# Key sums and query numerators over rows of four heads with both signs

## Chip, cores and metric

The kernel runs on one core of one Trainium2 chip. The metric is the device time of one execution in microseconds (us). Names of engines are those of the profile: PE (TensorE, matrix products; PEld are its weight loads), DVE (VectorE), ACT (ScalarE), POOL (GpSimd) and SP (SyncE, whose queue issues most transfers).

## The reference

Two mixers act on the same 2048 tokens of width 512, and a gate blends them. The diff touches mixer A, a linear attention with 32 heads of 16 channels.

```python
q, k, v = ...                  # x @ wqkv, split into 32 heads of 16
pq = einsum('bhsd,hdf->bhsf', q, w_phi)          # likewise pk from k
phi_q = concat([softmax(pq), softmax(-pq)], -1)  # 32 features; likewise phi_k
kv = einsum('bhsf,bhsd->bhfd', phi_k, v)         # summed over all tokens
z  = einsum('bhsf->bhf', phi_k)
num = einsum('bhqf,bhfd->bhqd', phi_q, kv)
den = einsum('bhqf,bhf->bhq', phi_q, z)[..., None] + 1e-06
a = (num / den) heads side by side @ wo
# mixer B: z = gelu(x @ w_in); z1, z2 = halves; z2 = layernorm(z2)
# b = (z1 * (w_sp @ z2 + b_sp)) @ w_out
out = g * a + (1 - g) * b      # g = sigmoid(sum(x * gate_w)), one per token
```

Every feature is a softmax over 16 values, once of the projection and once of its negative; key features are summed against v over all tokens before any query can be answered.

## The kernel before

Tokens come in NT = 16 tiles of 128. The order of work on every engine is the order of the program, written out by hand; tiles are followed by semaphores only. PSUM is one array ps of eight banks of 512 f32 columns, and the bank numbers are chosen by hand.

**First stage.** For each token tile, PE computes x @ w_in (z_piece, L174), ACT applies gelu, DVE takes the layer norm's statistics. In between come v_proj (v for a token tile, tokens on partitions, copied by ACT into vv) and fold, which multiplies w_phi into the q and k weights, so that wq and wk yield pq and pk at once. wv's columns are reordered first, heads innermost (permute_wv).

**First loop, i = 0 to 15.** gg_half(i) is one half of a spatial tile of mixer B: 16 matmuls of 344 columns (L370) into bank i % 2, which DVE multiplies into u (L378); after each second half, SP issues a transpose of u by DMA into uT, and a load of a further w_sp tile. k_norm(i) sums the exponentials ek of a token tile over the 16 values of each head (L319), inverts (L325), and multiplies v by the inverses, once for each sign (L327): it is v that is scaled, and ek stays as it is. kv_acc(i - 1) accumulates, for both signs and four groups of eight heads, 128 feature rows by 128 v columns and 8 sums of weights: eight matmuls of 136 columns (L343), in banks 3 to 5. k_proj(i + 2) computes pk of a token tile and both exponentials (L307, L312, L313). In the last four iterations q_proj yields pq for four token tiles at once, features on partitions (L397), with its exponentials.

**Second loop, j = 0 to 15.** One more gg_half, in all but the last two, which share one. q_num(j) uses q's exponentials as stationary operand against kvx, the masked key sums: eight matmuls of 144 columns (L417), of which 8 + 8 columns for each sign and group are q's own softmax sums and the denominators' parts. Twelve DVE instructions (L425 to L455) combine signs, denominators and gate into o, tokens on partitions; SP issues its transpose into oT (L457). out_tile(j - LAG), with LAG = 4, multiplies uT (L463) and oT (L468) by w_out and wo, ACT copies (L472), and SP issues the store (L473). The last tile is done in two halves.

Between the loops stand one gg_half, the last kv_acc and kv_extract (L348). That turns the sums in PSUM into kvx, with everything outside a head's own block masked away. A bank is written again only when its reader is done: gg_half's u, the exponentials, kv_extract, and in the second loop q_num's DVE instructions.

Of the kernel before, what the change touches and what calls it, by code (L numbers as in the profile page):

```python
# [37 lines left out]
def kernel(  # L38
# [47 lines left out]
    wv_n = pers.tile([P, NDT, D], BF16, name="wv_n")  # L86
# [9 lines left out]
    warm = vv[:, 13, :]  # L96
    nc.vector.memset(warm[:, 0:P], 0.0)
# [7 lines left out]
    xn = vv[:, 14:16, :]  # L105
# [12 lines left out]
        out=wv_n[:, :, :],  # L118
# [181 lines left out]
    KBANK = (2, 6)  # L300
    ek_t = {}
    vr_t = {}

    def k_proj(t):
        b = KBANK[t % 2]
        for dt in range(NDT):
            nc.tensor.matmul(  # L307
                ps[:, b, :], lhsT=xT[:, dt, t * P:(t + 1) * P], rhs=wk[:, dt, :],
                start=(dt == 0), stop=(dt == NDT - 1),
            )  # L310
# [4 lines left out]

    def k_norm(t):
        ek = ek_t[t]
        zk = ring2.tile([P, 2 * NDT, 8], FP32, name="zk")
        nc.vector.tensor_reduce(  # L319
            out=zk[:], in_=ek[:].rearrange("p a (g h f) -> p (a g) h f", g=NDT, h=8),  # L320
            axis=AX.X, op=ALU.add,
        )
        vr = ring2.tile([P, 2 * NDT, VW], BF16, name="vr")
        with nc.allow_low_precision(reason="the normalised feature is bf16 in the reference"):
            nc.vector.reciprocal(out=vr[:, :, P:VW], in_=zk[:])  # L325
        for a in range(2):
            nc.vector.tensor_tensor(  # L327
                out=vr[:, a * NDT:(a + 1) * NDT, 0:P].rearrange("p g (d h) -> p g d h", h=8),
                in0=vv[:, t, :].rearrange("p (g d h) -> p g d h", g=NDT, h=8),
                in1=vr[:, a * NDT:(a + 1) * NDT, None, P:VW].to_broadcast([P, NDT, DH, 8]),  # L330
                op=ALU.mult,
            )
        vr_t[t] = vr
# [4 lines left out]

    def kv_acc(t):
        ek, vr = ek_t.pop(t), vr_t.pop(t)  # L340
        for j in range(2 * NDT):
# [1 line left out]
            nc.tensor.matmul(  # L343
                kv_slot(j), lhsT=ek[:, a, g * P:(g + 1) * P], rhs=vr[:, j, :],
                start=(t == 0 and j % 3 == 0), stop=(t == NT - 1), skip_group_check=True,
            )

    def kv_extract():  # L348
        for b in range(3):
            n = 3 if b < 2 else 2  # L350
            acc = ps[:, 3 + b, 0:n * VW].rearrange("p (n w) -> p n w", w=VW)
            j = 3 * b
            nc.vector.scalar_tensor_tensor(
                out=kvx[:, j:j + n, P:VW], in0=acc[:, :, P:VW], scalar=0.5 * DEN_EPS,
                in1=mask16[:, None, :].to_broadcast([P, n, 8]), op0=ALU.add, op1=ALU.mult,
            )
            for i in range(n):
                nc.vector.tensor_tensor(
                    out=kvx[:, j + i, 0:P].rearrange("p (h d) -> p h d", h=8),
                    in0=acc[:, i, 0:P].rearrange("p (d h) -> p h d", h=8),  # L360
                    in1=mask16[:, :, None].to_broadcast([P, 8, DH]), op=ALU.mult,
                )
# [26 lines left out]
    def e_buf(c):  # L389
        if c % 2 == 0:  # L390
            return wqkT[:].rearrange("p (a g) n -> p a g n", a=2)
        return vv[:, 0:8, :].rearrange("p (a g) n -> p a g n", a=2)

    def q_proj(c, g):
        e = e_buf(c)
        for dt in range(NDT):
# [8 lines left out]
    oT_t = {}

    def n_slot(a, g):
        if g < 3:
            return ps[:, 3 + a, g * QW:(g + 1) * QW]
        return ps[:, 5, a * QW:(a + 1) * QW]  # L410

    def q_num(t):
        c, i = divmod(t, CH // P)
        e = e_buf(c)
        for g in range(NDT):
            for a in range(2):
                nc.tensor.matmul(  # L417
                    n_slot(a, g), lhsT=e[:, a, g, i * P:(i + 1) * P],
                    rhs=kvx[:, a * NDT + g, :], start=True, stop=True,
                )  # L420
        main = ps[:, 3:5, 0:3 * QW].rearrange("p a (g w) -> p a g w", w=QW)
        last = ps[:, 5, 0:2 * QW].rearrange("p (a w) -> p a w", w=QW)
        sd = ring2.tile([P, 2, NDT, 16], FP32, name="sd")
        for a in range(2):
            nc.vector.tensor_copy(out=sd[:, a, 0:3, :], in_=main[:, a, :, P:QW])  # L425
        nc.vector.tensor_copy(out=sd[:, :, 3, :], in_=last[:, :, P:QW])
        tw = ring2.tile([P, 4, NDT, 8], FP32, name="tw")
        for a in range(2):
            nc.vector.tensor_tensor(
                out=tw[:, a], in0=sd[:, a, :, 0:8], in1=sd[:, 1 - a, :, 8:16], op=ALU.mult  # L430
            )
        nc.vector.tensor_tensor(out=tw[:, 2], in0=tw[:, 0], in1=tw[:, 1], op=ALU.add)
        nc.vector.reciprocal(out=tw[:, 3], in_=tw[:, 2])
        w = ring2.tile([P, 2, NDT, 8], FP32, name="w")
        for a in range(2):
            nc.vector.scalar_tensor_tensor(
                out=w[:, a], in0=sd[:, 1 - a, :, 8:16], scalar=gate[:, t:t + 1],
                in1=tw[:, 3], op0=ALU.mult, op1=ALU.mult,
            )
        pr = ring2.tile([P, 2, D], BF16, name="pr")  # L440
        for a in range(2):
            nc.vector.tensor_tensor(  # L442
                out=pr[:, a, 0:3 * P].rearrange("p (g h d) -> p g h d", g=3, d=DH),
                in0=main[:, a, :, 0:P].rearrange("p g (h d) -> p g h d", d=DH),
                in1=w[:, a, 0:3, :, None].to_broadcast([P, 3, 8, DH]),
                op=ALU.mult,
            )
        nc.vector.tensor_tensor(
            out=pr[:, :, 3 * P:D].rearrange("p a (h d) -> p a h d", d=DH),
            in0=last[:, :, 0:P].rearrange("p a (h d) -> p a h d", d=DH),  # L450
            in1=w[:, :, 3, :, None].to_broadcast([P, 2, 8, DH]),
            op=ALU.mult,
        )
# [133 lines left out]
```

## Time and profile before

| | us |
|---|---|
| median of three runs (217.18 to 217.5) | 217.28 |
| profiled execution, whole | 217.18 |
| its span, first to last instruction | 215.4 |
| PE busy | 209.2 |
| DVE busy | 152.1 |
| ACT busy | 81.3 |
| first stage, until the first gg_half | 0 to 61 |
| first loop and kv_acc(15) | 61 to 124 |
| second loop and the last tiles | 124 to 215.4 |

Busy shares are averages over these stages. In the profile's groups a row names line, engine, operation, output and inputs, shape and count; behind the bar stand busy us and the mean ns of one, and behind the second bar the idle time before, with what ended it. A matmul's recorded duration contains its way through the array; the pitch from one matmul to the next is shorter and is read from the chain or the timeline. The granted PE clock is 0.998 of full speed as a mean.

### The profile page before, as it was taken

What the parts mean: (1) busy time and instruction counts of PE and PEld (TensorE: products, weight loads), DVE (VectorE), ACT (ScalarE), POOL (GpSimd) and SP (SyncE); (2) the same over time, 40 slices, a digit from 0 to 9 for tenths busy, and PEclk for the clock granted to TensorE, in tenths of its full rate; (3) what the DMA queues carried; (4) which work ended last, traced back from release to release, by engine and by line L of the source; (5) the groups of instructions that cost most, each with busy time, mean ns of one, the idle gap of its engine ahead of it and who ended that gap; (6) DMA issues with size and microseconds to landing.
All of it is one profiled execution on the core that took longest, in us unless ns stands there. A gap on an engine that the chain in (4) does not pass through costs nothing.

```text
span 215.4 us, 3615 instructions
## 1 busy us (share of the span) xinstructions
PE 209.2 (97%) x1364; PEld 125.2 (58%) x1388; DVE 152.1 (71%) x462; ACT 81.3 (38%) x141; POOL 1.9 (1%) x13
## 2 busy tenths in 40 slices
PE   7999999999999999999999999999999999999994
PEld 6355555554456666666656666655555665565543
DVE  2279757395969887878777799997666666679900
ACT  2356676865773242424245222322332223311222
POOL 3000000000000000000000000000000000000000
PEclk9999999999999999999999999999999999999999
DMA  6999999990001464646338261422312313242341
GB/s 188 262 212 212 188 210 201 189 283 18 0 3 37 97 137 75 97 101 134 64 73 134 47 123 27 84 56 59 87 49 55 82 49 62 49 73 64 91 117 52
DMA packets 73441, 22.30 MB, mean 103 GB/s; under 512 B 67744, under 2 KB 73424, under 8 KB 73424
## 3 DMA queue, kind: packets, MB, share of 16 engines
q1 hardware_dynamic: 72208, 21.48, 47.9%
q10 hardware_dynamic: 1216, 0.59, 1.0%
q8 instruction: 11, 0.18, 0.4%
q14 instruction: 6, 0.05, 0.1%
HBM read 3.44 MB, written 2.10 MB: 26 GB/s over the span
## 4 chain that ended last, share of the span: by engine, by line
PE 92%; DMA 3%; DVE 1%; issue 1%; SPq 1%; ACT 0%
PE ps L370 34%; PE ps L174 16%; PE ps L463 10%; PE ps L266 6%; PE ps L307 6%; PE ps L468 6%; PE ps L397 6%; PE ps L417 4%; PE ps L343 4%; DMA w_in<-in_B_w_in_dram 3%; PE ps L293 1%; DVE pr L442 0%; DVE u L378 0%; SPq L110 0%; SPq L108 0%
## 5 line engine op out<-in xcount | busy, mean ns | idle before, releaser
L370 PE MATMUL ps<-zz,wsp 128*128 128x344 bf16 x512 | 80.1, 309 | 0.1
L370 PEld LDWEIGHTS <-wsp 128*128 128x128 bf16 x512 | 50.1, 98 | 28.9
L174 PE MATMUL ps<-w_in,xT 128*128 128x512 bf16 (+1 forms) x188 | 39.5, 360 | 0.7 <-DMA w_in<-in_B_w_in_dram 0.5
L378 DVE SCALAR_TENSOR_TENSOR u<-ps,bcol,zz 128x344 bf16<-128x344 f32 x32 | 18.4, 575 | 27.8 <-PE ps L370 27.7
L174 PEld LDWEIGHTS <-xT 128*128 128x128 bf16 x192 | 18.5, 99 | 19.1 <-DMA w_in<-in_B_w_in_dram 1.0
L199 ACT ACTIVATE zz<-ps 128x1376 bf16<-128x1376 f32 (+2 forms) x18 | 21.4, 1190 | 20.8 <-PE ps L174 20.8
L208 DVE BATCH_NORM_STATS2 stats<-zz 128x6 f32<-128x344 bf16 x32 | 14.9, 507 | 15.0 <-ACT zz L199 15.0
L463 PE MATMUL ps<-w_out,uT 128*128 128x512 bf16 (+1 forms) x100 | 23.4, 366 | 0.1
L312 ACT ACTIVATE ek<-ps 128x512 bf16<-128x512 f32 x16 | 9.6, 598 | 34.5 <-PE ps L307 34.4
L472 ACT ACTIVATE ob<-ps 128x512 bf16<-128x512 f32 (+1 forms) x17 | 9.7, 572 | 29.7 <-PE ps L468 22.1
L319 DVE TENSOR_REDUCE zk<-ek 128x64 f32<-128x1024 bf16 x16 | 19.3, 1209 | 0.0
L307 PE MATMUL ps<-wk,xT 128*128 128x512 bf16 x57 | 15.9, 379 | 0.4
L442 DVE TENSOR_TENSOR pr<-ps,w 128x384 bf16<-128x384 f32 x32 | 16.2, 549 | 0.0
L468 PE MATMUL ps<-wo,oT 128*128 128x512 bf16 (+1 forms) x65 | 16.1, 366 | 0.1
L397 PE MATMUL ps<-xT,wq 128*128 128x512 bf16 x58 | 15.8, 379 | 0.3
L463 PEld LDWEIGHTS <-uT 128*128 128x128 bf16 x102 | 9.8, 98 | 10.0
L266 PE MATMUL ps<-wv,xT 128*128 128x512 bf16 x62 | 15.5, 379 | 0.1
L402 ACT ACTIVATE vv<-ps 128x512 bf16<-128x512 f32 x8 | 4.8, 598 | 25.7 <-PE ps L397 25.7
L327 DVE TENSOR_TENSOR vr<-vv,vr 128x512 bf16<-128x512 bf16 x32 | 12.2, 422 | 0.6
L402 ACT ACTIVATE wqkT<-ps 128x512 bf16<-128x512 f32 x8 | 4.8, 599 | 17.4 <-PE ps L397 17.4
L468 PEld LDWEIGHTS <-oT 128*128 128x128 bf16 x68 | 6.7, 98 | 7.2
L343 PE MATMUL ps<-vr,ek 128*128 128x136 bf16 x128 | 10.2, 223 | 0.0
(62 smaller groups left out, 182.9 us busy)
## 6 DMA issues: line engine op xcount, KB each, us to landing
out_dram<-ob SPq DMA_DIRECT2D x15, 128.0 KB, 1.9
w_out<-in_B_w_out_dram SPq DMA_DIRECT2D x1, 640.0 KB, 5.7
w_in<-in_B_w_in_dram ACTq DMA_DIRECT2D x2, 256.0 KB, 3.8
w_in<-in_B_w_in_dram SPq DMA_DIRECT2D x1, 512.0 KB, 5.4
wv_n<-in_A_wqkv_dram SPq DMA_DIRECT2D x1, 512.0 KB, 6.0
wo<-in_A_wo_dram SPq DMA_DIRECT2D x1, 512.0 KB, 6.0
w_in<-in_B_w_in_dram SPq DMA_DIRECT2D x1, 352.0 KB, 6.8
vv<-in_A_x_dram SPq DMA_DIRECT2D x2, 128.0 KB, 3.1
```

The lines of the kernel that those rows point to most:

```text
L174: nc.tensor.matmul(zb[:, n0:n1], lhsT=xT[:, dt, t * P:(t + 1) * P], rhs=w_in[:, dt, n0:n1], start=(dt == 0), stop=(dt == NDT - 1),)
L199: nc.scalar.activation(out=zz[:, t, n0:n1], in_=zbank(t)[:, n0:n1], func=AF.Gelu_apprx_tanh)
L266: nc.tensor.matmul(ps[:, b, :], lhsT=xT[:, dt, t * P:(t + 1) * P], rhs=wv[:, dt, :], start=(dt == 0), stop=(dt == NDT - 1),)
L307: nc.tensor.matmul(ps[:, b, :], lhsT=xT[:, dt, t * P:(t + 1) * P], rhs=wk[:, dt, :], start=(dt == 0), stop=(dt == NDT - 1),)
L319: nc.vector.tensor_reduce(out=zk[:], in_=ek[:].rearrange("p a (g h f) -> p (a g) h f", g=NDT, h=8), axis=AX.X, op=ALU.add,)
L343: nc.tensor.matmul(kv_slot(j), lhsT=ek[:, a, g * P:(g + 1) * P], rhs=vr[:, j, :], start=(t == 0 and j % 3 == 0), stop=(t == NT - 1), skip_ ...
L370: nc.tensor.matmul(ps[:, b, 0:HF], lhsT=wsp[:, tt % WSLOTS, s, :], rhs=zz[:, s, FH + h * HF:FH + (h + 1) * HF], start=(s == 0), stop=(s == ...
L378: nc.vector.scalar_tensor_tensor(out=u[:, h * HF:(h + 1) * HF], in0=ps[:, b, 0:HF], scalar=bcol[:, tt:tt + 1], in1=zz[:, tt, h * HF:(h + 1 ...
L397: nc.tensor.matmul(ps[:, 7, :], lhsT=wq[:, dt, g * P:(g + 1) * P], rhs=xT[:, dt, c * CH:(c + 1) * CH], start=(dt == 0), stop=(dt == NDT - 1),)
L442: nc.vector.tensor_tensor(out=pr[:, a, 0:3 * P].rearrange("p (g h d) -> p g h d", g=3, d=DH), in0=main[:, a, :, 0:P].rearrange("p g (h d) ...
L463: nc.tensor.matmul(ps[:, b, n0:n1], lhsT=uT[:, ft, :], rhs=w_out[:, ft, n0:n1], start=(ft == 0), stop=False,)
L468: nc.tensor.matmul(ps[:, b, n0:n1], lhsT=oT[:, g, :], rhs=wo[:, g, n0:n1], start=False, stop=(g == NDT - 1),)
```

## The change

A row of four heads now takes both signs: 4 x 16 features of the positive and 4 x 16 of the negative exponential are the 128 rows of a product, and there are eight such groups instead of four groups times two signs.

- Key features themselves are normalised, in place (norm): sum, reciprocal, product over all 1024 features of a token. v is no longer scaled or reordered; vv gets a column of ones beside each group of 64 channels. kv_acc has eight matmuls of 65 columns, into eight slots in banks 3 and 4.
- q is projected like k, one token tile at a time with tokens on partitions (feat), normalised by the same norm, and transposed by a DMA on SP's queue (128 x 1024 into eT). q_num has eight matmuls of 68 columns, and signs add up inside the product. A reciprocal of 32 and one product remain on DVE.
- Order: q_proj runs three tiles ahead and q_norm two; three extra gg_half in the first loop after i = 3, 7, 11 and one more in each of its last three iterations leave ten for the second loop, in two of three iterations. out_tile follows three tiles behind. Its stores, but for the first half of the last tile, are issued by ACT.
- Space: exponentials lie in w_in (five slots) and xn (one), eT in wqkT, uT has 16 buffers.

```diff
-VW = P + 8
-QW = P + 16
+NHG = 8
+HW = 4 * DH
+VP = HW + 2
+QW = HW + 4
 WSLOTS = 8
-LAG = 4
+LAG = 3
+QAHEAD = 3
...
-    vv = pers.tile([P, NT, D], BF16, name="vv")
+    vv = pers.tile([P, NT, NHG, VP], BF16, name="vv")
...
-    kvx = pers.tile([P, 2 * NDT, QW], BF16, name="kvx")
+    kvx = pers.tile([P, NHG, QW], BF16, name="kvx")
...
-    wv_n = pers.tile([P, NDT, D], BF16, name="wv_n")
+    mask4 = pers.tile([P, 4], BF16, name="mask4")
+    xn = pers.tile([P, 2, D], BF16, name="xn")
+    warm = pers.tile([P, P], BF16, name="warm")
...
-    warm = vv[:, 13, :]
-    nc.vector.memset(warm[:, 0:P], 0.0)
+    nc.vector.memset(warm[:], 0.0)
...
     nc.sync.dma_start(
-        out=wv_n[:, :, :],
+        out=wv[:, :, :],
         in_=A_wqkv[:, 2 * D:3 * D].rearrange("(dt p) n -> p dt n", p=P),
...
-    nc.vector.tensor_copy(
-        out=kvx[:, :, VW:QW], in_=mask16[:, None, :].to_broadcast([P, 2 * NDT, 8])
-    )
+    nc.gpsimd.memset(vv[:, :, :, HW:VP], 1.0)
+    nc.vector.tensor_tensor(out=mask4[:], in0=mask16[:, 0:4], in1=mask16[:, 4:8], op=ALU.add)
...
-        nc.scalar.activation(out=vv[:, t, :], in_=ps[:, b, :], func=AF.Copy)
...
+        nc.scalar.activation(
+            out=vv[:, t, :, 0:HW], in_=ps[:, b, :].rearrange("p (g n) -> p g n", g=NHG),
+            func=AF.Copy,
+        )
...
+    QBANK = (5, 7)
     ek_t = {}
-    vr_t = {}
+    eq_t = {}
+    w_in_flat = w_in[:].rearrange("p d f -> p (d f)")
+
+    def e_slot(i):
+        if i == 5:
+            flat = xn[:].rearrange("p t d -> p (t d)")
+        else:
+            flat = w_in_flat[:, i * 2 * D:(i + 1) * 2 * D]
+        return flat.rearrange("p (g a n) -> p g a n", g=NHG, a=2)
+
+    def feat(t, w, b, e):
+        for dt in range(NDT):
+            nc.tensor.matmul(
+                ps[:, b, :], lhsT=xT[:, dt, t * P:(t + 1) * P], rhs=w[:, dt, :],
+                start=(dt == 0), stop=(dt == NDT - 1),
+            )
+        src = ps[:, b, :].rearrange("p (g n) -> p g n", g=NHG)
+        for a, sc in enumerate((1.0, -1.0)):
+            nc.scalar.activation(out=e[:, :, a, :], in_=src, func=AF.Exp, scale=sc)
+
+    def norm(e):
+        ev = e.rearrange("p g a (h f) -> p (g a h) f", h=4)
+        zs = ring2.tile([P, 2 * H], FP32, name="zs")
+        nc.vector.tensor_reduce(out=zs[:], in_=ev, axis=AX.X, op=ALU.add)
+        rs = ring2.tile([P, 2 * H], FP32, name="rs")
+        nc.vector.reciprocal(out=rs[:], in_=zs[:])
+        nc.vector.tensor_tensor(
+            out=ev, in0=ev, in1=rs[:, :, None].to_broadcast([P, 2 * H, DH]), op=ALU.mult
+        )
 
     def k_proj(t):
-        b = KBANK[t % 2]
-        for dt in range(NDT):
-            nc.tensor.matmul(
-                ps[:, b, :], lhsT=xT[:, dt, t * P:(t + 1) * P], rhs=wk[:, dt, :],
-                start=(dt == 0), stop=(dt == NDT - 1),
-            )
-        ek = ring3.tile([P, 2, D], BF16, name="ek")
-        nc.scalar.activation(out=ek[:, 0, :], in_=ps[:, b, :], func=AF.Exp, scale=1.0)
-        nc.scalar.activation(out=ek[:, 1, :], in_=ps[:, b, :], func=AF.Exp, scale=-1.0)
-        ek_t[t] = ek
+        ek_t[t] = e_slot(t % 3)
+        feat(t, wk, KBANK[t % 2], ek_t[t])
...
     def k_norm(t):
-        ek = ek_t[t]
...
+        norm(ek_t[t])
+
+    def q_proj(t):
+        eq_t[t] = e_slot(3 + t % 3)
+        feat(t, wq, QBANK[t % 2], eq_t[t])
+
+    eT_t = {}
+
+    def q_norm(t):
+        e = eq_t.pop(t)
+        norm(e)
+        eT = wqkT[:, 2 * (t % 4):2 * (t % 4) + 2, :].rearrange("p a (b n) -> p (a b) n", n=P)
+        nc.sync.dma_start_transpose(out=eT, in_=e.rearrange("p g a n -> p (g a n)"))
+        eT_t[t] = eT
+
+    slots = ps[:, 3:5, :].rearrange("p b (c w) -> p (b c) w", w=P)
...
     def kv_acc(t):
-        ek, vr = ek_t.pop(t), vr_t.pop(t)
...
+        ek = ek_t.pop(t)
+        for g in range(NHG):
+            nc.tensor.matmul(
+                slots[:, g, 0:HW + 1], lhsT=ek[:, g, :, :].rearrange("p a n -> p (a n)"),
+                rhs=vv[:, t, g, 0:HW + 1],
+                start=(t == 0 and g % 4 == 0), stop=(t == NT - 1), skip_group_check=True,
             )
...
     def kv_extract():
...
+        nc.vector.tensor_tensor(
+            out=kvx[:, :, 0:HW].rearrange("p g (h d) -> p g h d", h=4),
+            in0=slots[:, :, 0:HW].rearrange("p g (h d) -> p g h d", h=4),
+            in1=mask4[:, None, :, None].to_broadcast([P, NHG, 4, DH]), op=ALU.mult,
+        )
+        nc.vector.scalar_tensor_tensor(
+            out=kvx[:, :, HW:QW], in0=slots[:, :, HW:HW + 1].to_broadcast([P, NHG, 4]),
+            scalar=0.5 * DEN_EPS, in1=mask4[:, None, :].to_broadcast([P, NHG, 4]),
+            op0=ALU.add, op1=ALU.mult,
+        )
...
     def q_num(t):
...
+        eT = eT_t.pop(t)
+        for g in range(NHG):
+            nc.tensor.matmul(
+                slots[:, g, 0:QW], lhsT=eT[:, g, :], rhs=kvx[:, g, :], start=True, stop=True
+            )
+        rd = ring2.tile([P, NHG, 4], FP32, name="rd")
+        nc.vector.reciprocal(out=rd[:], in_=slots[:, :, HW:QW])
         o = ring2.tile([P, D], BF16, name="o")
-        nc.vector.tensor_tensor(out=o[:], in0=pr[:, 0, :], in1=pr[:, 1, :], op=ALU.add)
+        nc.vector.scalar_tensor_tensor(
+            out=o[:].rearrange("p (g h d) -> p g h d", g=NHG, h=4),
+            in0=slots[:, :, 0:HW].rearrange("p g (h d) -> p g h d", h=4),
+            scalar=gate[:, t:t + 1],
+            in1=rd[:, :, :, None].to_broadcast([P, NHG, 4, DH]), op0=ALU.mult, op1=ALU.mult,
+        )
         oT = oTpool.tile([P, NDT, P], BF16, name="oT")
         nc.sync.dma_start_transpose(out=oT[:, :, :], in_=o[:, :])
         oT_t[t] = oT
...
     def out_tile(t):
         ob = ring3.tile([P, D], BF16, name="ob")
         if t < NT - 1:
-            out_part(t, (2, 6)[t % 2], 0, D, ob, nc.sync)
+            out_part(t, (2, 6)[t % 2], 0, D, ob, nc.scalar)
...
-    uTpool = ctx.enter_context(tc.tile_pool(name="uTp", bufs=12))
+    uTpool = ctx.enter_context(tc.tile_pool(name="uTp", bufs=NT))
...
-    permute_wv()
...
+    gg_next = 0
+
+    def gg(n):
+        nonlocal gg_next
+        for _ in range(n):
+            gg_half(gg_next)
+            gg_next += 1
+
     for i in range(NT):
-        gg_half(i)
+        gg(1)
         k_norm(i)
         if i >= 1:
             kv_acc(i - 1)
         if i + 2 < NT:
             k_proj(i + 2)
-        if i >= NT - 4:
-            q_proj(0, i - (NT - 4))
-
-    gg_half(NT)
+        if i >= NT - QAHEAD:
+            q_proj(i - (NT - QAHEAD))
+        if i > NT - QAHEAD:
+            q_norm(i - (NT - QAHEAD) - 1)
+        if i in (3, 7, 11) or i >= NT - QAHEAD:
+            gg(1)
+
     kv_acc(NT - 1)
     kv_extract()
-    gg_done = NT + 1
+    q_norm(QAHEAD - 1)
     for j in range(NT):
-        if gg_done < 2 * NT - 1:
-            gg_half(gg_done)
-            gg_done += 1
-        elif j == NT - 2:
-            gg_half(gg_done, 0, NT // 2)
-        else:
-            gg_half(gg_done, NT // 2, NT)
+        if j % 3 < 2 and gg_next < 2 * NT:
+            gg(1)
         q_num(j)
-        if j + 4 < NT:
-            c, g = divmod(j + 4, NDT)
-            q_proj(c, g)
+        if j + QAHEAD < NT:
+            q_proj(j + QAHEAD)
+        if 1 <= j and j + QAHEAD - 1 < NT:
+            q_norm(j + QAHEAD - 1)
         if j >= LAG:
             out_tile(j - LAG)
     for j in range(NT - LAG, NT):
         out_tile(j)
```

More of the change, by code (lines that the diff above doesn't have):

```diff
@@ L104 @@
     w_in_v = B_w_in.rearrange("(dt p) f -> p dt f", p=P)
-    xn = vv[:, 14:16, :]
     nc.sync.dma_start(out=xn[:, 0, :], in_=x2[0:P, :])
@@ L269, in v_proj @@
             )
-        nc.scalar.activation(out=vv[:, t, :], in_=ps[:, b, :], func=AF.Copy)
-    def permute_wv():
-        for dt in range(NDT):
-            nc.vector.tensor_copy(
-                out=wv[:, dt, :].rearrange("p (g d h) -> p g d h", g=NDT, d=DH),
-                in_=wv_n[:, dt, :].rearrange("p (g h d) -> p g d h", g=NDT, d=DH),
-            )
+        nc.scalar.activation(
+            out=vv[:, t, :, 0:HW], in_=ps[:, b, :].rearrange("p (g n) -> p g n", g=NHG),
+            func=AF.Copy,
+        )
     def build_wphi():
@@ L300 @@
     KBANK = (2, 6)
+    QBANK = (5, 7)
     ek_t = {}
-    vr_t = {}
-    def k_proj(t):
-        b = KBANK[t % 2]
+    eq_t = {}
[7 more added lines that the diff above has]
+    def feat(t, w, b, e):
         for dt in range(NDT):
             nc.tensor.matmul(
-                ps[:, b, :], lhsT=xT[:, dt, t * P:(t + 1) * P], rhs=wk[:, dt, :],
+                ps[:, b, :], lhsT=xT[:, dt, t * P:(t + 1) * P], rhs=w[:, dt, :],
@@ L309, in k_proj @@
                 start=(dt == 0), stop=(dt == NDT - 1),
             )
-        ek = ring3.tile([P, 2, D], BF16, name="ek")
-        nc.scalar.activation(out=ek[:, 0, :], in_=ps[:, b, :], func=AF.Exp, scale=1.0)
-        nc.scalar.activation(out=ek[:, 1, :], in_=ps[:, b, :], func=AF.Exp, scale=-1.0)
-        ek_t[t] = ek
-    def k_norm(t):
-        ek = ek_t[t]
[L318 to L333, printed above, removed]
@@ L335, in kv_slot @@
-    def kv_slot(j):
-        b, c = divmod(j, 3)
-        return ps[:, 3 + b, c * VW:(c + 1) * VW]
+        src = ps[:, b, :].rearrange("p (g n) -> p g n", g=NHG)
[10 more added lines that the diff above has]
+        )
@@ new lines, in k_proj @@
+    def k_proj(t):
+        ek_t[t] = e_slot(t % 3)
+        feat(t, wk, KBANK[t % 2], ek_t[t])
+    def k_norm(t):
+        norm(ek_t[t])
[9 more added lines that the diff above has]
+        eT_t[t] = eT
@@ L339, in kv_acc @@
+    slots = ps[:, 3:5, :].rearrange("p b (c w) -> p (b c) w", w=P)
     def kv_acc(t):
-        ek, vr = ek_t.pop(t), vr_t.pop(t)
-        for j in range(2 * NDT):
-            a, g = divmod(j, NDT)
+        ek = ek_t.pop(t)
+        for g in range(NHG):
             nc.tensor.matmul(
-                kv_slot(j), lhsT=ek[:, a, g * P:(g + 1) * P], rhs=vr[:, j, :],
-                start=(t == 0 and j % 3 == 0), stop=(t == NT - 1), skip_group_check=True,
+                slots[:, g, 0:HW + 1], lhsT=ek[:, g, :, :].rearrange("p a n -> p (a n)"),
+                rhs=vv[:, t, g, 0:HW + 1],
+                start=(t == 0 and g % 4 == 0), stop=(t == NT - 1), skip_group_check=True,
@@ L346, in kv_acc @@
             )
     def kv_extract():
[L349 to L362, printed above, removed]
+        nc.vector.tensor_tensor(
[3 more added lines that the diff above has]
+        )
@@ L387, in gg_half, with q_num @@
                 load_wsp(tt + WSLOTS)
[L389 to L396, printed above, removed]
+    oT_t = {}
+    def q_num(t):
+        eT = eT_t.pop(t)
+        for g in range(NHG):
             nc.tensor.matmul(
-                ps[:, 7, :], lhsT=wq[:, dt, g * P:(g + 1) * P],
-                rhs=xT[:, dt, c * CH:(c + 1) * CH],
-                start=(dt == 0), stop=(dt == NDT - 1),
-            )
-        nc.scalar.activation(out=e[:, 0, g, :], in_=ps[:, 7, :], func=AF.Exp, scale=1.0)
-        nc.scalar.activation(out=e[:, 1, g, :], in_=ps[:, 7, :], func=AF.Exp, scale=-1.0)
@@ L405 @@
[L405 to L416, printed above, removed]
-                nc.tensor.matmul(
[L418 to L452, printed above, removed]
-        )
-        o = ring2.tile([P, D], BF16, name="o")
-        nc.vector.tensor_tensor(out=o[:], in0=pr[:, 0, :], in1=pr[:, 1, :], op=ALU.add)
@@ new lines, in q_num @@
+                slots[:, g, 0:QW], lhsT=eT[:, g, :], rhs=kvx[:, g, :], start=True, stop=True
+            )
+        rd = ring2.tile([P, NHG, 4], FP32, name="rd")
+        nc.vector.reciprocal(out=rd[:], in_=slots[:, :, HW:QW])
+        o = ring2.tile([P, D], BF16, name="o")
+        nc.vector.scalar_tensor_tensor(
[3 more added lines that the diff above has]
+            in1=rd[:, :, :, None].to_broadcast([P, NHG, 4, DH]), op0=ALU.mult, op1=ALU.mult,
+        )
```

## The prediction

> **What bounds the kernel now.** The page's busy shares and slices come first: is one engine full everywhere?
>
> ```profile
> span 215.4 us, 3615 instructions
> ...
> PE 209.2 (97%) x1364; PEld 125.2 (58%) x1388; DVE 152.1 (71%) x462; ACT 81.3 (38%) x141; POOL 1.9 (1%) x13
> ...
> PE   7999999999999999999999999999999999999994
> ...
> DVE  2279757395969887878777799997666666679900
> ...
> PE 92%; DMA 3%; DVE 1%; issue 1%; SPq 1%; ACT 0%
> ```
>
> TensorE (PE) is, and 92% of the chain that ended last is its own work. So a matmul saved is time saved, unless PE starts to wait; VectorE (DVE) is at seven to nine tenths in the middle, the nearest to a second bound. Then the groups of instructions, shapes kept apart, for durations (the last two numbers before the second bar: busy us, ns of one):
>
> ```profile
> L319 DVE TENSOR_REDUCE zk<-ek 128x64 f32<-128x1024 bf16 x16 | 19.3, 1209 | 0.0
> L378 DVE SCALAR_TENSOR_TENSOR u<-ps,bcol,zz 128x344 bf16<-128x344 f32 x32 | 18.4, 575 | 27.8 <-PE ps L370 27.7
> L442 DVE TENSOR_TENSOR pr<-ps,w 128x384 bf16<-128x384 f32 x32 | 16.2, 549 | 0.0
> ...
> L448 DVE TENSOR_TENSOR pr<-ps,w 128x256 bf16<-128x256 f32 x16 | 6.6, 414 | 0.0
> ...
> L280 DVE TENSOR_TENSOR wphi<-wphiW,mask 128x512 bf16<-128x512 bf16 x1 | 0.7, 698 | 0.0
> ```
>
> Next the timeline of one iteration of the first loop (start, duration, engine; brackets: idle before it):
>
> ```profile
> 119.66 0.64 PE L343 MATMUL ps<-vr,ek 128*128 128x136 bf16 x8
> 119.86 0.57 DVE L378 SCALAR_TENSOR_TENSOR u<-ps,bcol,zz 128x344 bf16<-128x344 f32 x1 [0.58 <-PE ps L370]
> ...
> 120.36 1.21 DVE L319 TENSOR_REDUCE zk<-ek 128x64 f32<-128x1024 bf16 x1
> ...
> 121.60 0.55 DVE L325 RECIPROCAL vr<-zk 128x64 bf16<-128x64 f32 x1
> ...
> 122.19 0.76 DVE L327 TENSOR_TENSOR vr<-vv,vr 128x512 bf16<-128x512 bf16 x2
> ...
> 123.33 0.64 PE L343 MATMUL ps<-vr,ek 128*128 128x136 bf16 x8
> ```
>
> The reader is to see how little air there is: PE repeats every 3.67 us, DVE is done at 122.95, and PE takes the result at 123.33, 0.38 later. Last, the transposes' time from issue to landing:
>
> ```profile
> uT<-u SPq DMA_TRANSPOSE x16, 2.8
> oT<-o SPq DMA_TRANSPOSE x16, 2.4
> ```
>
> **What it takes off PE.** From the chain in order of time: spatial half G = 2.33 (one gg_half, 16 matmuls), projection V = 0.86, output tile O = 1.29 + 0.86 = 2.15, kv_acc 0.47 (119.66 to 120.13), q_num 0.53. All counts stay; only kv_acc's and q_num's 2 x 128 matmuls go from 136 and 144 columns to 65 and 68. No row has so few. Pitch of 512 columns is 0.86/4 = 215 ns, of 344 it is 2.33/16 = 146, so 0.41 ns a column: streaming alone makes 27 ns at 65. The weight load stays 128x128, and the folding matmuls of 128 columns run every 55 ns with it (0.8% of the chain over 32): that is the upper end. I take the middle, 41 ns: 0.33 for kv_acc, 0.34 for q_num, 16 x (0.14 + 0.19) = 5.3 us off (at 27 ns 9, at 55 ns 1.7).
>
> The Trainium skill's "TensorE: Matmul & The Clock Gate", section "Back-to-back issue gap", gives about 81 ns for each pair of weight load and 128-column matmul in a real kernel; by it these 256 would take 21 us, 5 more than now. The trace disagrees: 55 ns.
>
> **What it costs on DVE.** k_norm keeps the reduction (1.24 to the next start) and the reciprocal (0.59), and its two products of 0.42 become one of 1024 elements. L442 and L448 give 1.055 ns an element over 0.144, so 1.22 us. Lower end 0.70, by L327's bf16 rate (512 in 0.422); upper end 1.25, by L280, all bf16 but with one operand held still over 16 elements, as here. I take 1.22, since the new factor is f32 and held still too. A normalisation then lasts 3.05 us, and frees DVE after 2.98 (independent instructions overlap by 0.07). There are now 32, 16 of them for q, where q_num's 12 small instructions (3.6 us a tile) become a reciprocal of 32 (0.35) and one product from PSUM of 512 (0.21 + 1.055 x 0.512 = 0.75). DVE from 61 us on: 32 x 2.98 + 32 x 0.50 + 16 x 1.1 + 0.9 = 130 us, beside 145.5 us of PE. It fits in sum; what matters is where it bunches. kv_extract falls from 2.3 (124.02 to 126.3) to 0.9 us.
>
> **The walk.** Time runs as in the trace of before; u starts 0.20 after PE moves on; I allow 0.06 from DVE's end to PE. I follow PE through each wait.
> First loop: kv_acc(i) needs norm(i), which ends 0.20 + 0.50 + 3.05 + 0.06 = 3.81 after gg's end; PE is back there after 2.33 + 0.33 + 0.86 = 3.52. It waits 0.29, which moves the next gg back, so the next one is in time: 0.29 in every second iteration, none where a second gg follows (i = 3, 7, 11). First wait (no kv_acc before it) 0.62, then six of 0.29: 2.4 us.
> i = 14 and 15: DVE has two normalisations and two u, 6.96, against PE's 5.85. A gg waits 0.25 for its bank, kv_acc(15) 1.15 for norm(15): 1.4 us. kv_acc(15) ends at 136.1.
> Start of the second loop: DVE still has q_norm(1) and u, then kv_extract to 140.0, q_norm(2) to 143.0, u, o(0) to 144.6. gg ends at 138.4, q_num(0) waits 1.64 for kv_extract; q_num(1) 1.09 for o(0), which reads the same two banks; q_num(2) and (3) 0.5 each for o(1), o(2), behind q_norm(3) and (4). q_num(3) needs eT(3) besides: norm done at 149.4 and a transpose, at 152.6: 2.16 more. Sum 5.9 us. From then on three tiles cost DVE 13.2 us and PE 14.7 (out_tile has joined), and no wait is left until the end.
> Tail: with gg used up, q_num(13) ends at 202.8; DVE does o(13), norm(15), o(14): q_num(15) is reached at 207.5, waits 0.96 for o(14), then 2.16 for eT(15). Then three output tiles cover oT(15) (1.1 + 2.4 against 6.45): 3.1 us.
> A transpose of eight 128-column blocks: four land in 2.4, six in 2.8, so 3.2. Lower end 2.8; upper end 4.5, the longest uT and oT in the trace.
> Waits: 2.4 + 1.4 + 5.9 + 3.1 = 12.8 us; less 5.3, PE ends 7.4 later (with rounding), at 219.6, span 222.8. Against the profiled execution, 217.18 (1.78 around its span): 224.6. It lies 0.10 below the median, less than I can tell.
>
> **Costed at nothing.** permute_wv goes (2.2 us of DVE) and mask4 comes: PE leads there, DVE is busy 38 of 51 us; uncovered, 2.2 us gained. POOL's new memset of vv (w_out's of 512 took 0.52) is 60 us early. Both exponentials stay 0.60. The stores of output tiles go to ACT: some 0.5 us of issue each, ACT then 2.2 us of 3.3 or more per tile; if ACT were full, 0.5 a tile. SP gains 16 issues of some 1.3 us (uT 1.22) and loses 15 stores; eT stands behind oT, whose source DVE makes first, so it delays nothing.
>
> **Rivals.**
> *Packed multiply (other side).* The 1024-element product at 0.70: norm(i) is 0.52 sooner, loop waits vanish, kv_extract and o still cost 2.5, eT 4.3. Time 218.7 at 41 ns, 216.0 at 28; at 41 ns it turns faster only from 0.44 us down, at 28 ns from 0.83 down. L280 speaks against it.
> *Matmuls no narrower.* 55 ns a matmul: 1.7 us gained, waits 11.4: 226.8. For it: the weight load is unchanged. Against: nothing shows the load itself takes 55.
> *Late landings.* Three streams of transposes in SP's queue; at 4.5 us the two eT waits recur and sum to 9.5 instead of 4.3, o's shrink: 228.3. For: maxima of 4.5. Against: medians near the minimum.
> *The clock falls.* The tail pause is 3.1 us in one piece. At the start the same matmul of 128 columns ran every 106 ns (24 in 2.74 us), later every 55: half speed after idleness. Half speed for 3.4 to 6.8 us of the 8.6 us left costs 1.7 to 3.4: 226.3 to 228.0. Against: the pause may be shorter. The Trainium skill, same page, section "What's actually happening", states that the clock halves after an idle window of about 3.4 us; no run here shows where the limit lies.
>
> **Chances.** The walk 0.56 (221.5 at 27 ns and 2.8 us, to 226); matmuls no narrower 0.13; late landings 0.12; clock 0.04; packed multiply 0.08, half of it faster; unforeseen 0.07 (0.03 faster, 0.02 the same, 0.02 slower). The measurement can tell about 0.2%, 0.43 us. Faster 0.07, same 0.02, slower 0.91. The likeliest gives 224.6; the range, 219.5 to 229.5, goes down towards the packed multiply and up past late landings (228.3) to landings late with matmuls at 55 ns (229.7), leaving out some 0.1 below and less above.
>
> **What would show it.** Right: the reduction unchanged and the product near 1.22; PE waits on DVE at kv_acc; PE's idle time in two lumps, 136 to 153 us and near the end; fewer PE busy us. Wrong: a product near 0.7, narrow matmuls over 60 ns or under 27, eT landing under 2.5, or PE full to the end.

## The result and the profile after

The changed kernel is slower: 226.98 us median (225.9 to 229.01, four runs) against 217.26, a ratio of 1.0456 with a 95% interval of 1.0377 to 1.0535. The prediction was 224.6 us, range 219.5 to 229.5. The profiled execution took 227.59 us, 225.9 of it the span. Medians here are of all runs of a kernel, ratios of those within 1.5% of its fastest run.

The page of the changed kernel, the lines that answer to those shown of the kernel before, and the granted PE clock:

```profile
span 225.9 us, 3549 instructions
...
PE 208.0 (92%) x1388; PEld 117.2 (52%) x1388; DVE 166.1 (74%) x305; ACT 81.4 (36%) x141; POOL 2.2 (1%) x14
...
PE   7799999999999999999999977759999999998494
...
DVE  2258585586969979979875899998798988989100
...
PEclk9999999999999999999999999997999999999889
...
PE 65%; DVE 21%; DMA 8%; issue 3%; SPq 1%; ACT 0%; DVEq 0%
```

PE is no longer full: it has holes in the slices at 130 to 152 us and at 209 to 215. DVE now has 21% of the chain that ended last (1% before) and the transfers 8% (3%). Right behind the first hole and around the second (152 to 158 us, 209 to 220) the clock's digit falls below 9, which it never did before.

The groups of the changed kernel, shapes kept apart:

```profile
L327 DVE TENSOR_TENSOR w_in<-w_in,rs 128x1024 bf16<-128x1024 bf16 x27 | 33.1, 1224 | 0.9
L324 DVE TENSOR_REDUCE zs<-w_in 128x64 f32<-128x1024 bf16 x27 | 32.6, 1209 | 0.0
...
L410 DVE SCALAR_TENSOR_TENSOR o<-ps,st,rd 128x512 bf16<-128x512 f32 x16 | 12.0, 751 | 0.6
...
L404 PE MATMUL ps<-kvx,wqkT 128*128 128x68 bf16 x128 | 6.9, 197 | 9.5 <-DMA wqkT<-w_in 6.6 <-DVE kvx L368 1.4 <-DVE o L410 1.3
...
L356 PE MATMUL ps<-vv,w_in 128*128 128x65 bf16 x128 | 6.8, 194 | 2.6 <-DVE w_in L327 2.6
```

DVE's durations are those of the walk: 1224, 1209 and 751 ns. The two groups of narrow matmuls are the ones that wait: kv_acc (L356) for the normalised features, q_num (L404) for the transpose into eT (which lies in wqkT), for kvx and for o.

The two holes in the timeline. First the start of the second loop, PE's part:

```profile
135.38 0.43 PE L356 MATMUL ps<-vv,w_in 128*128 128x65 bf16 x8 [0.97 <-DVE w_in L327]
...
139.54 0.41 PE L404 MATMUL ps<-kvx,wqkT 128*128 128x68 bf16 x8 [1.39 <-DVE kvx L368]
...
144.05 0.42 PE L404 MATMUL ps<-kvx,wqkT 128*128 128x68 bf16 x8 [0.90 <-DVE o L410]
...
145.70 0.41 PE L404 MATMUL ps<-kvx,wqkT 128*128 128x68 bf16 x8 [0.37 <-DVE o L410]
...
151.89 0.63 PE L404 MATMUL ps<-kvx,wqkT 128*128 128x68 bf16 x8 [2.58 <-DMA wqkT<-w_in]
...
152.34 1.90 PE L313 MATMUL ps<-wq,xT 128*128 128x512 bf16 x4
```

Then the end, with the queues:

```profile
207.90 1.23 SPq L348 DMA_TRANSPOSE wqkT<-w_in  x1
...
208.69 0.34 ACTq L433 DMA_DIRECT2D out_dram<-ob  x1
...
212.01 0.43 PE L404 MATMUL ps<-kvx,wqkT 128*128 128x68 bf16 x8 [3.98 <-DMA wqkT<-w_in]
...
212.28 1.88 PE L423 MATMUL ps<-w_out,uT 128*128 128x512 bf16 x6
...
213.95 1.91 PE L428 MATMUL ps<-wo,oT 128*128 128x512 bf16 x4
```

These are the waits of the walk, in its order and nearly its sizes. The brackets count idleness from the modelled end of the last matmul. The walk counts from the time at which PE could have started the next one, which is some 0.16 us earlier. Counted like the walk, from the start times, the waits are 1.12 (1.15 forecast), 1.56 (1.64), 1.05 (1.09), 0.53 (0.5), 2.74 (0.5 + 2.16). The last is 4.15 where 0.96 + 2.16 was forecast. What no step of the walk has is what stands behind the two long pauses: four matmuls of 512 columns take 1.90 instead of 1.03 us. Granted clock by stages of this trace: 1.00 until 135.4 us, 0.92 from 135.4 to 156.0, 1.00 to 207.9, 0.82 from 207.9 to 217.6, then 1.00 again.

### The profile page after: what moved, and what is told of

Same layout as the page of the kernel before. It is cut to its first block, busy times and chain, and to the rows that moved or that the text cites. A ratio compares the mean times of both kernels' runs of the same rounds, so it can differ in the third digit from the quotient of the medians.

```text
span 225.9 us, 3549 instructions
## 1 busy us (share of the span) xinstructions
PE 208.0 (92%) x1388; PEld 117.2 (52%) x1388; DVE 166.1 (74%) x305; ACT 81.4 (36%) x141; POOL 2.2 (1%) x14
## 3 DMA queue, kind: packets, MB, share of 16 engines
q10 hardware_dynamic: 3376, 2.56, 3.5%
## 4 chain that ended last, share of the span: by engine, by line
PE 65%; DVE 21%; DMA 8%; issue 3%; SPq 1%; ACT 0%; DVEq 0%
PE ps L380 19%; PE ps L176 15%; PE ps L423 9%; PE ps L313 7%; DVE zs L324 7%; PE ps L268 6%; PE ps L428 6%; DVE w_in L327 5%; DVE rs L326 3%; DMA wqkT<-w_in 3%; DMA w_in<-in_B_w_in_dram 3%; DVE u L388 3%; DMA wqkT<-xn 2%; PE ps L404 2%; PE ps L356 1%
## 5 line engine op out<-in xcount | busy, mean ns | idle before, releaser
L319 ACT ACTIVATE w_in<-ps 128x512 bf16<-128x512 f32 x54 | 29.1, 596 | 81.0 <-PE ps L313 81.0
L327 DVE TENSOR_TENSOR w_in<-w_in,rs 128x1024 bf16<-128x1024 bf16 x27 | 33.1, 1224 | 0.9
L324 DVE TENSOR_REDUCE zs<-w_in 128x64 f32<-128x1024 bf16 x27 | 32.6, 1209 | 0.0
L176 PEld LDWEIGHTS <-xT 128*128 128x128 bf16 x192 | 18.3, 98 | 19.5 <-DMA w_in<-in_B_w_in_dram 1.3
L423 PE MATMUL ps<-w_out,uT 128*128 128x512 bf16 (+1 forms) x102 | 24.9, 383 | 0.0
L326 DVE RECIPROCAL rs<-zs 128x64 f32<-128x64 f32 x32 | 17.7, 553 | 1.1
L313 PE MATMUL ps<-wq,xT 128*128 128x512 bf16 x64 | 17.3, 394 | 0.0
L404 PE MATMUL ps<-kvx,wqkT 128*128 128x68 bf16 x128 | 6.9, 197 | 9.5 <-DMA wqkT<-w_in 6.6
L313 PEld LDWEIGHTS <-xT 128*128 128x128 bf16 x128 | 10.8, 98 | 8.7 <-issue 0.6
L404 PEld LDWEIGHTS <-wqkT 128*128 128x128 bf16 x128 | 6.1, 99 | 13.2 <-DMA wqkT<-w_in 7.4
L410 DVE SCALAR_TENSOR_TENSOR o<-ps,st,rd 128x512 bf16<-128x512 f32 x16 | 12.0, 751 | 0.6
```

The costliest lines, as they stand in the source:

```text
L176: nc.tensor.matmul(zb[:, n0:n1], lhsT=xT[:, dt, t * P:(t + 1) * P], rhs=w_in[:, dt, n0:n1], start=(dt == 0), stop=(dt == NDT - 1),)
L313: nc.tensor.matmul(ps[:, b, :], lhsT=xT[:, dt, t * P:(t + 1) * P], rhs=w[:, dt, :], start=(dt == 0), stop=(dt == NDT - 1),)
L319: nc.scalar.activation(out=e[:, :, a, :], in_=src, func=AF.Exp, scale=sc)
L324: nc.vector.tensor_reduce(out=zs[:], in_=ev, axis=AX.X, op=ALU.add)
L326: nc.vector.reciprocal(out=rs[:], in_=zs[:])
L327: nc.vector.tensor_tensor(out=ev, in0=ev, in1=rs[:, :, None].to_broadcast([P, 2 * H, DH]), op=ALU.mult)
```

## Experiments

Times are medians; before is 217.3 us beside each of them, and the changed kernel 226.98. Theory A is that of the prediction, with the half pace behind long pauses added.

**The narrow matmuls alone.** In the kernel before, only the columns of kv_acc and q_num are cut:

```diff
-                kv_slot(j), lhsT=ek[:, a, g * P:(g + 1) * P], rhs=vr[:, j, :],
+                kv_slot(j)[:, VW - 65:VW], lhsT=ek[:, a, g * P:(g + 1) * P], rhs=vr[:, j, VW - 65:VW],
...
-                    n_slot(a, g), lhsT=e[:, a, g, i * P:(i + 1) * P],
-                    rhs=kvx[:, a * NDT + g, :], start=True, stop=True,
+                    n_slot(a, g)[:, QW - 68:QW], lhsT=e[:, a, g, i * P:(i + 1) * P],
+                    rhs=kvx[:, a * NDT + g, QW - 68:QW], start=True, stop=True,
```

> The kernel before, with only the matmuls of kv_acc and q_num cut to 65 and 68 columns (the last ones of each group, so most of the products with v are left out); weight loads, VectorE and all else as before. It prices the narrowing alone. Theory A (from the changed kernel's trace: eight such matmuls take 0.25 us instead of 0.47 and 0.53): 16 x (0.22 + 0.28) = 8.0 us less, of which about 1 may be lost where q_num of the first tiles then meets VectorE: 209.3 to 210.3 us against 217.3. Rival B (the weight load bounds narrow matmuls, 55 ns each): 1.7 us less, 215.6 us.

Measured: 210.84 us, ratio 0.9705 (0.9682 to 0.9729), 6.5 us less. Rival B is out. Eight of these matmuls take 0.24 to 0.25 us up to the next start, 31 ns each. The rest of the 8.0 us meets DVE in the first tiles of the second loop, a little more of it than allowed. Start times of q_num(1) and q_num(2) in this run, and the DVE product between that reads the same banks:

```profile
125.96 0.59 PE L417 MATMUL ps<-kvx,wqkT 128*128 128x68 bf16 x8
...
128.86 1.02 DVE L442 TENSOR_TENSOR pr<-ps,w 128x384 bf16<-128x384 f32 x2
129.59 0.89 PE L417 MATMUL ps<-kvx,wqkT 128*128 128x68 bf16 x8
```

q_num now starts while DVE is still at it, and is stretched from 0.41 to 0.89 us. So the kernel before had little room left there itself. (This kernel leaves out most products with v, so it prices time alone.)

**DVE's load.** The product of q's normalisation is left out (`norm(e, False)` in q_norm skips the last instruction of norm).

> The changed kernel without the product of q's normalisation (1.22 us on VectorE for each of 16 tiles; q's features stay unnormalised); the sums, reciprocals and transposes stay. Theory A (VectorE's backlog makes TensorE wait): by the walk from wait to wait, with 31 ns a matmul, 5.5 us less: 1.1 off kv_acc(15) and the u bank, 1.2 off kv_extract, 2.6 off the product o, 0.6 off eT; the last pause (a transpose's landing) stays. 221.5 us, or 1.7 less if the pause at 152 us gets too short to cost the clock. Rival D (the transposes' landing makes the waits, VectorE is only near): at most 1 us less, 226 us.

Measured: 218.97 us in ten runs, ratio to before 1.0048 (1.0018 to 1.0078), 8.0 us less than the changed kernel. Rival D is out: 1.22 us off each q tile on DVE takes the waits for kvx away, leaves 0.60 of those for o, and halves the first wait for eT. The remaining waits of q_num in this run:

```profile
PE ps L405 <- DMA wqkT<-w_in: 3.4, 2, 2.0
...
PE ps L405 <- DVE o L411: 0.6, 1, 0.6
```

It is 2.5 us more than the walk's 5.5. In the trace the first wait for eT is now 1.33 us and full pace follows it. The last pause, which the expectation left as it was, shrinks from 3.98 to 2.03 us; half pace still follows it. The ten runs fall into two groups, six from 218.96 to 219.20 and four from 217.03 to 217.33; the 1.9 us between them is about the price of one stretch at half pace (1.7 below). The granted clock agrees: 0.992 in each of the six, 1.000 in each of the four.

**Half pace behind a pause.** Idle matmuls fill three pauses of the changed kernel. In the first try they write unused columns of bank 0:

```diff
+    def fill(j):
+        for _ in range({0: 22, 3: 40, NT - 1: 62}.get(j, 0)):
+            nc.tensor.matmul(
+                ps[:, 0, HF:HF + P], lhsT=warm[:, 0:P], rhs=warm[:, 0:P], start=True, stop=True
+            )
...
+        fill(j)
         q_num(j)
```

> The changed kernel, with idle matmuls of 128 columns (55 ns each, into columns of bank 0 that nothing reads) put ahead of q_num(0) (22), q_num(3) (40) and q_num(15) (62), shorter than TensorE's pauses there (1.4, 2.6 and 4.0 us). Theory A: the matmuls behind the pauses at 152 and 212 us run at half pace because TensorE had been idle; kept busy it keeps its clock: about 1.7 us less behind each, 3.4 less in all, some 223.6 us, a granted clock near 0.998, and less scatter from run to run. Rival C (the half pace has nothing to do with the pause, or lies in the trace alone): no change, 227 us.

Measured: 235.75 us as the median of four; the ratio, 1.0764 (1.0692 to 1.0837), is that of the two runs of 232.66 and 235.1 us. By these it is some seven slower than the changed kernel, which neither theory expected. The trace names the reason, a fault of the experiment:

```profile
142.87 2.50 PE L513 MATMUL ps<-warm 128*128 128x128 bf16 x22 [4.85 <-DVE u L388]
...
159.45 4.42 PE L513 MATMUL ps<-warm 128*128 128x128 bf16 x40 [3.87 <-DVE u L388]
...
219.06 3.63 PE L513 MATMUL ps<-warm 128*128 128x128 bf16 x62
...
222.77 1.46 PE L423 MATMUL ps<-w_out,uT 128*128 128x512 bf16 x5
```

Sharing a bank with u's source made the first two groups wait for u, which DVE does last; after 4.9 and 3.9 us of idleness they ran at 107 ns instead of 55. The third group waited for nothing and kept PE busy, and the output tile behind it ran at full pace. So the second try uses a bank that is long free:

```diff
-                ps[:, 0, HF:HF + P], lhsT=warm[:, 0:P], rhs=warm[:, 0:P], start=True, stop=True
+                ps[:, 2 if j < NT - 1 else 0, 0:P], lhsT=warm[:, 0:P], rhs=warm[:, 0:P], start=True, stop=True
```

> As e2_fill, but the idle matmuls go to a bank whose last reader is long done (bank 2 ahead of q_num(0) and q_num(3), bank 0 ahead of q_num(15)): in e2_fill the first two groups waited for u (3.9 and 4.9 us), the last did not wait, and behind it the output tiles ran at full pace. Theory A (idleness of TensorE costs the clock): nothing is delayed, and both stretches at half pace go: about 1.7 us less each, 223.6 us, granted clock near 0.998. Rival C: 227 us as the changed kernel, or more.

Measured: 224.63 us (224.37 to 225.22), ratio to before 1.0340 (1.0304 to 1.0376), 2.3 us less than the changed kernel and with a scatter of 0.9 instead of 3.1 us. Fill, q_num(3) and the projection behind it in this run:

```profile
149.24 2.40 PE L513 MATMUL ps<-warm 128*128 128x128 bf16 x40
152.18 0.43 PE L404 MATMUL ps<-kvx,wqkT 128*128 128x68 bf16 x8 [0.54 <-DMA wqkT<-w_in]
152.44 1.02 PE L313 MATMUL ps<-wq,xT 128*128 128x512 bf16 x3
```

This wait ends about when it ended before (152.18, then 151.89), but the matmuls behind it run at full pace, and the granted clock is 1.000. Adding work to PE makes the kernel faster: rival C is out. That the gain is 2.3 and not the 3.4 expected fits the clock of the changed kernel's four runs: 0.985 in two of them (227.59 and 229.01 us), but 0.992, as with one stretch at half pace, in the other two (225.9 and 226.36).

**Cover for the last transpose.** The last spatial halves are kept back:

```diff
-        if j % 3 < 2 and gg_next < 2 * NT:
+        if (j % 3 < 2 and j < 10) or j in (11, 13, NT - 1):
```

> The changed kernel with its last spatial halves kept back: in the second loop they come at j = 0, 1, 3, 4, 6, 7, 9, 11, 13 and 15 instead of 0, 1, 3, 4, 6, 7, 9, 10, 12 and 13; nothing else. Theory A: the pause of 4.0 us ahead of q_num(15) is covered but for some 0.9, and the half pace behind it (1.7) goes; the walk from wait to wait gives 2.3, with the landing as measured 3.1, so 3 to 5 us less: 222 to 224 us. Rival F (the last transpose lands late because it queues behind others, and moves with them): about 227 us.

Measured: 223.35 us (222.92 to 224.79), ratio 1.0291 (1.0245 to 1.0337), 3.6 us less than the changed kernel. Issue of the last eT transpose, and q_num(15), in this run:

```profile
205.11 1.23 SPq L348 DMA_TRANSPOSE wqkT<-w_in  x1
...
209.23 0.43 PE L404 MATMUL ps<-kvx,wqkT 128*128 128x68 bf16 x8 [1.66 <-DMA wqkT<-w_in]
209.50 1.46 PE L423 MATMUL ps<-w_out,uT 128*128 128x512 bf16 x5
```

The pause shrinks from 3.98 to 1.66 us and no half pace follows: rival F is out. The transpose itself takes 4.1 us as before; it is only covered. Nor does half pace follow the pause at 150 us, which has 2.56 us here as in the changed kernel's trace (2.58): whether such a pause costs the clock differs from run to run.

**Why the last transpose lands late.** It takes 4.1 us where the median of the sixteen is 3.2. The store of out_tile(11) is issued 0.8 us behind it; here that store waits for the next tile's.

```diff
+        if t == NT - 5:
+            late.append((t, ob))
+            return
         dma.dma_start(out=out2[t * P:(t + 1) * P, n0:n1], in_=ob[:, n0:n1])
+        while late:
+            t0, ob0 = late.pop()
+            dma.dma_start(out=out2[t0 * P:(t0 + 1) * P, :], in_=ob0[:])
```

> The changed kernel with one store held back: that of out_tile(11), which ACT issues 0.8 us after the last eT transpose and so while it is under way, is issued behind that of out_tile(12) instead. Read from the trace, not the time: from the issue of the last eT transpose to q_num(15). Theory H (a plain store under way beside the transpose makes it land in 4.1 instead of 3.2 us): about 3.2 us. Rival I (the store has no part in it; the transpose of o behind it, or the transfer itself, takes the time): 4.0 us or more as before.

The last transpose and q_num(15) in this run:

```profile
208.56 1.23 SPq L348 DMA_TRANSPOSE wqkT<-w_in  x1
...
211.91 0.64 PE L404 MATMUL ps<-kvx,wqkT 128*128 128x68 bf16 x8 [3.22 <-DMA wqkT<-w_in]
```

3.35 us instead of 4.11, in one trace: theory H. The other traces go with it: in the run with cover for the last transpose, the store is again issued 0.8 us behind, and the transpose takes 4.1; in the next run the store is issued 1.3 us behind, and it takes 3.1. Two runs of this kernel took 224.78 and 228.85 us, which says nothing about its time. Undoing the move of the stores altogether (`nc.sync` in out_tile in place of `nc.scalar`) says the same:

> The changed kernel with all stores of output tiles issued by SP again, as in the kernel before: this part of the change undone alone. Costed at nothing: within the changed kernel's own scatter, 226 to 229 us. Rival J (SP then waits for ob with the next transposes queued behind it): eT and oT are issued later, one or more us slower.

Measured: 224.93 us (223.24 to 227.01), ratio 1.0377 (1.0320 to 1.0434). The lower end is that of the runs without half pace, and the interval meets the changed kernel's, so a gain is not shown; a loss of 1 us or more is excluded, and with it rival J. From its issue to q_num(15) the last transpose takes 3.1 us (206.23 to 209.31); the store now stands behind it in the same queue.

**Which pauses cost the clock.** The traces on hand settle what the runs above left open, without a run made for it. In the changed kernel the granted clock is one half from 151.74 to 155.15 us and from 213.18 to 216.59. Both stretches last 3.41 us, and the 58.03 us between them are 17 times 3.41: the clock changes on a grid of 3.41 us. The table cuts the traces by that grid, which each shows by its own clock changes.

| run | window, us | PE idle in it, us | clock in the next |
|---|---|---|---|
| changed kernel | 148.33 to 151.74 | 2.43 | half |
| changed kernel | 206.36 to 209.77 | 1.74 | full |
| changed kernel | 209.77 to 213.18 | 2.24 | half |
| without q's product | 201.35 to 204.76 | 2.03 | half |
| last halves kept back | 147.26 to 150.67 | 1.22 | full |
| last halves kept back | 150.67 to 154.09 | 1.39 | full |
| stores on SP | 204.78 to 208.20 | 1.80 | full |
| stores on SP | 208.20 to 211.61 | 1.11 | full |

So the length of the pause does not decide, but how much of it falls into one window. The pause of 2.92 us with the stores on SP is split over two windows and costs nothing, while 2.03 us in one window cost 1.7. The runs with the late store (2.4 us idle in each of two windows) and with the first fill (3.3 and 2.8) agree: half pace follows all four. In these traces the limit lies between 1.80 and 2.03 us of a window. The grid lies differently against the kernel in each execution, so the same pause can cost the clock in one and not in the next.

**Another order.** The same instructions as in the changed kernel, behind the first stage in this order (gg a spatial half; kn, ka, kp k_norm, kv_acc, k_proj; qp, qn q_proj, q_norm; kx kv_extract; num q_num):

```diff
+    ORDER = """
+    kn0 gg kn1 qp0 gg kp2 ka0 kp3 kn2 gg gg ka1 kn3 kp4 ka2 gg kp5 ka3 kn4 kp6 kn5 gg
+    ka4 gg kp7 kn6 ka5 kn7 qp1 kp8 gg kn8 ka6 kp9 gg ka7 gg kp10 ka8 kn9 gg qp2 kn10
+    kp11 kn11 ka9 gg ka10 gg kp12 qn0 ka11 gg kp13 kn12 gg kn13 kp14 gg kn14 ka12 gg
+    kp15 gg kn15 ka13 gg qn1 gg qn2 qp3 ka14 ka15 gg gg kx qp4 qn3 qp5 gg num0 gg num1
+    qn4 gg num2 out0 qp6 qn5 qn6 qp7 num3 gg gg out1 num4 qn7 qp8 out2 num5 qn8 qp9 out3
+    out4 num6 qn9 qp10 out5 qp11 num7 out6 qn10 num8 gg qp12 qn11 gg num9 out7 qp13 qn12
+    num10 qn13 qp14 gg gg num11 qn14 qp15 out8 num12 out9 out10 qn15 out11 num13 gg
+    num14 out12 num15 out13 out14 out15
+    """
```

> The changed kernel with the same instructions in another order behind the first stage, nothing added or left out: q's projections and normalisations are spread from early in the first loop on, two to three tiles ahead of q_num, the spatial halves are spread over both loops, one or two of them near the end. Theory A (only the bunching on VectorE and the lack of cover for the last transposes cost time): hardly any wait on TensorE, no half pace: span about 207 to 210, time 209 to 212 us, below the kernel before. Rival E (VectorE, with 130 us of work in the last 160, or the third stream of transposes, bounds whatever the order): 217 us or more.

Measured: 210.17 us (209.73 to 210.69), ratio to before 0.9674 (0.9647 to 0.9700): faster than both kernels, by 7.1 us than the one before. Its page:

```profile
span 208.6 us, 3530 instructions
...
PE   7799999999999999999999999999999999999993
...
DVE  1157758466798989998999979989999899998520
...
PE 91%; DMA 5%; issue 1%; SPq 1%; ACT 0%
```

DVE is as busy as in the changed kernel (165.3 us) and no longer in the chain. Rival E is out: DVE's sum never was the limit, its bunching was. In this order, norms of k run ahead of kv_acc by more than one spatial half, q's normalisations alternate with halves, and q_num finds its eT landed.

**The packed multiply.** On top of that order, the factor rs is bf16 (`name="rs"` with BF16 in place of FP32):

> e4_order with the reciprocals rs in bf16 instead of f32, so that all operands of the product of 1024 have two bytes. It prices the rival of the packed multiply. Theory A (the factor is held still over 16 elements, and this alone keeps the product at one element a step, as 128x512 in 698 ns in the kernel before): 1.22 to 1.25 us as before, 210.2 us. Rival G (the f32 factor keeps it slow): 0.70 us a product, 32 x 0.5 = 17 us off VectorE, and 208.5 to 210 us, since TensorE hardly waits any more.

Measured: 209.83 us, ratio to before 0.9656 (0.9633 to 0.9679), not to be told from the order alone, and within what both theories allow. The product's own duration tells them apart:

```profile
L328 DVE TENSOR_TENSOR w_in<-w_in,rs 128x1024 bf16<-128x1024 bf16 x27 | 33.1, 1225 | 1.0
```

It takes 1225 ns, as with the f32 factor. Rival G is out: with all operands of two bytes the product stays at the rate of the row L280 of the kernel before. The Trainium skill's "VectorE: DVE Perf Modes", section "What auto-detection actually checks", asks for 16-bit tensors with a step of plus or minus one; the factor's step is zero over 16 elements, and this run agrees.

## Why the prediction was right, and what was off

Each step against the runs.

- *Narrow matmuls, 41 ns, 5.3 us off PE.* Direction right, size too small: 31 ns, 8.0 us. The lower end of the bracket (27) was the nearer one; the unchanged weight load bounds nothing at this width. Put into the walk, 31 instead of 41 ns takes only 1.7 us off the end (221.1 instead of 222.8), since PE then comes earlier to the same waits.
- *DVE's durations.* Product 1.22, reduction 1.21, reciprocal 0.55, o 0.75, kv_extract 0.86 (0.9): all as worked out from the rows of before. The packed multiply is excluded by the last run.
- *First loop, 0.62 once and every second kv_acc late by 0.29, 2.4 us.* Shown: the trace has a wait on DVE at the first kv_acc and at six more, every second one except around the extra halves. By the start times they are 0.70 and six of 0.34 to 0.36, 2.8 us; with PE earlier by the narrower matmuls, each was bound to be a little longer.
- *Bunching at i = 14, 15 and the start of the second loop, 7.3 us with the last kv_acc.* Right within 0.15 at each wait, counted as the walk counts (the wait for u's bank, 0.25 forecast, is 0.37). The run without q's product and the one with another order show that DVE's queue is the cause.
- *Tail, 3.1 us.* Measured 4.15, or 3.98 by the bracket. The term too small is the landing, 4.1 instead of 3.2, and the run with the held-back store, 3.35, points to the store. The step that failed is the one that costed the stores' move to ACT at nothing: I priced ACT's time and SP's queue, not the transfer running beside a transpose.
- *The clock, held at a chance of 0.04.* This is the main miss of the central value in the profiled execution. Half pace did come, and at two places: behind 151.9 us the three pieces up to 156.0 took 4.15 us (0.63, 1.71 and 1.81 in the chain) instead of 0.25, 0.86 and 1.29, and behind 212 us 1.72, 1.71 and 1.72 instead of 1.29, 0.86 and 1.29. That is 1.7 us each. The rival spoke of the tail alone, with a pause of 3.1 us. A pause of 2.58 was enough in one trace and 2.03 in another, while 2.56 and 2.92 were not enough; the grid of windows above sorts them. The Trainium skill's "TensorE: Matmul & The Clock Gate", section "What's actually happening", gives a window of about 3.4 us that runs freely; the grid of 3.41 us agrees with such a window, but idleness of 2.03 us in one window costs the clock here too, and the measurement decides.

Sum: the walk's 222.8, less 1.7 for the matmuls, plus 0.9 for the landing, plus 3.4 for the clock, is 225.4; the span was 225.9. The order of the causes stands: the change saves PE some 8 us and loses some 15 to waits and 3 more to the clock. By what ended them, half of the 15 us are waits for DVE, whose work comes bunched, and half are waits for transposes with nothing to cover them. That the central value came within 2.4 us of the median is in part luck: with the matmuls at 31 ns it would have been 1.7 lower, and the clock's price, which it left out, is partly hidden by that.

Left open: why the transposes of eT issued at 131.4 and 172.8 us took 4.4 us each. A transpose of u was issued 1.3 and 1.6 us behind them, and in the second case a store 0.8 us ahead, but others with the same neighbours landed in 3.2 and 2.8 us. Only the second cost time, 0.3 us. So a store issued beside a transpose is not the only thing that delays one.

## What to carry to other kernels

A change that takes work off the bound engine and puts more on the next one is judged by where that work bunches, not by its sum: follow the second engine's queue from wait to wait, and if the sum fits, look for an order before giving the change up (here 226.98 became 210.17 with the same instructions). A pause of two to three microseconds on TensorE can cost 1.7 us more behind it, depending on where it falls. A transfer that is cheap to issue can still delay a transpose that somebody waits for.

## What the runs showed of the hardware

- Matmuls with a 128x128 weight load follow each other at 31 to 33 ns for 65 or 68 columns, 55 to 56 for 128, 59 for 136.
- The granted clock changes on a grid of 3.41 us. Behind a window of it in which PE was idle for 2.03 us or more, matmuls ran at half pace, 427 ns for 512 columns and 107 for 128, for 3.41 us; windows at full pace with 1.80 us or less of idleness were followed by full pace. In the kernels with the first fill and the late store half pace lasted for two windows, 6.83 us, in places. Idle matmuls of 128 columns in the pause prevented it.
- Idle matmuls into other columns of a PSUM bank that DVE still had to read were made to wait for that read, in this kernel's way of following tiles.
- A transpose within SBUF by DMA lands in 2.4 us for 128x512 and 2.5 to 2.8 for 128x768 (medians). For 128x1024 it is 2.7 to 3.4 in thirteen of the changed kernel's sixteen and 4.1 to 4.5 in three; the last of them, with a store of 128 KB issued 0.8 us behind it, took 4.1, and 3.3 with that store held back.
